# Nystromformer attention and multiplicative FFN: padded q tiles for the rest of A's scores, one load for the first w3 block, constants made at once, a q/k ring of four, and new due times

## The chip, the cores and the metric

The kernel runs on one core of a Trainium2 chip. A time is the device time of one execution, in microseconds; the time of a kernel is the median of its runs. The core has five engines with an instruction stream each: TensorE (PE in the profile; PEld is its weight load), VectorE (DVE), ScalarE (ACT), GpSimd (POOL) and SyncE (SP), which here only issues DMAs. GpSimd and, for the last stores, ScalarE issue DMAs too. Each stream is executed in its own order, and semaphores tie the streams together.

## The reference

Batch 8, 8 heads, sequence 576, head size 64, 32 landmarks. The result of the attention, 4608 tokens by 512, goes through a feed-forward block without a nonlinearity but with an elementwise product.

```python
q_lm = q.reshape(B, H, 32, 18, D).mean(axis=3)       # landmarks: means over 18 rows
k_lm = k.reshape(B, H, 32, 18, D).mean(axis=3)
A  = softmax(q @ k_lm.T / 8)                         # 576 x 32
Bm = softmax(q_lm @ k_lm.T / 8)                      # 32 x 32
C  = softmax(q_lm @ k.T / 8)                         # 32 x 576
Z  = Bm.T / (norm_1(Bm) * norm_inf(Bm) + 1e-6)
for _ in range(6):
    Z = 2 * Z - Z @ Bm @ Z
x  = (A @ Z @ C @ v)                                 # heads side by side: 4608 x 512
out = ((x @ w1) * (x @ w2)) @ w3 @ w_out             # 512 -> 1024 -> 1024 -> 512
```

## The kernel before, in words

**Work.** The kernel never forms x. It multiplies w3 by w_out once ("w34", 1024 x 512) and, for each batch, folds w1 and w2 into the small matrix Z C v ("U"), so that the dense part needs two products only: A times U (d1_mm, 768 products of 192 columns) and the elementwise product of its two halves times w34 (d2_mm, mostly of 512 columns).

**A quad** n (16 of them) is four heads of a batch: n = 2b + qd. For each quad, GpSimd issues two DMAs that load q and k and cast them to 16 bits into a tile "nat" (load_qk, L415); VectorE transposes both halves in blocks of 32 into Tq and Tk (trans, L444); the landmark means are made on TensorE for the first two quads (mean_mm) and on GpSimd for the others (mean_a, mean_b, mean_c, L452 to L467), turned into lmT (L490). Then come C's scores (s_mm) with Bm's scores beside them, A's scores (a_mm), softmaxes and A's transposition (a_trans, a_copy). The 576 rows of a head are 32 landmarks times 18 rows r; a_mm takes r = 0 to 15 in four groups of four rows, so 128 columns of Tq each. Two rows are left over, r = 16 and 17. For the two quads of a batch a_rest does them together (L239 with tile wide<-lmT,Tq, shape 128*64): four products, each on half of the array's columns, quad 0 into the lower and quad 1 into the upper half of the output's partitions, two accumulation steps each.

**A lane** g (pair_tasks) takes two batches: softmax of Bm, its norms, five iterations (it_mm, it_sq, it_out), Z, and the small product W. u_tasks makes U from W and the weights w1 and w2, which GpSimd loads (load_w12, L436).

**w34.** w3 comes in eight blocks of 512 KB (load_w3, L315), w_out in eight chunks of 256 KB (load_wout, L310), all issued by SyncE. A block is transposed on TensorE (w3_tr, L333), split into a high and a low 16-bit part by ScalarE (L340) and VectorE (L347); a chunk is split likewise (L320, L325); then 24 products of 512 columns per block follow, in groups of three for each chunk c (w34_mm, tiles bank<-wo,u). The first block is loaded and transposed in pieces of 1, 3 and 4 column groups, the others in halves of 4.

**Constants.** const_a (VectorE, zeros) and const_b (GpSimd, cb: the 128 x 128 identity) come first. const_c (VectorE, masks and ones, L273 to L284) must not start before 6.0 in the planner's time; const_d (ScalarE, L287 to L291) follows it. const_e are GpSimd's zero fills of v tiles (L296).

**Order.** A list scheduler (class Plan) writes all streams' order when the kernel is built. Each task has an engine, an estimated duration, dependencies, ring slots that it takes and frees, a due time ("prio") and sometimes an earliest time ("after"). On each engine the task that could start first is taken; among tasks that could start together, that with the lowest due time. On TensorE, a task in the array shape that is in use gets a bonus (MP for the full array, MT for the tiled shapes "64x32", "128x32", "32x32", "128x64"), because a change of shape costs INTO and OUT. The due times come from T0 + PER * b for the dense work of batch b, from att(n) for quads, lane(g) for lanes, cvt(b) for C times v, UO for U, p0 for a w3 block. Rings: six PSUM banks, six nat tiles, four Tq tiles and others.

Of the kernel before, what the change touches and what calls it, by code (L numbers as in the profile page):

```python
# [25 lines left out]
MT = 12.0  # L26
# [15 lines left out]
class Plan:  # L42
# [48 lines left out]
    def run(self):  # L91
# [15 lines left out]
        while len(order) < n:  # L107
            best = None
            for e, cand in avail.items():
# [7 lines left out]
                if not opts:  # L117
# [4 lines left out]
                    o[1].prio - ((MP if mode == "full" else MT) if e == "PE" and o[1].mode == mode else 0.0)))  # L122
# [43 lines left out]
def kernel(  # L166
# [13 lines left out]

    fixed = ctx.enter_context(tc.tile_pool(name="fixed", bufs=1))
# [14 lines left out]
    nats = slots(fixed, 6, [128, 2, GRP, D], FP16, "nat")  # L196
    Tqs = slots(fixed, 4, [128, GRP, M, 2], FP16, "Tq")
# [15 lines left out]
    bscs = slots(fixed, 2, [128, 4, 32], FP32, "bsc")  # L213
    wTs = slots(fixed, 2, [128, 2, 256], FP16, "wT")
    cvs = slots(fixed, 4, [128, 2, D], FP32, "cv")
    bms = slots(fixed, 2, [128, 4, 32], FP32, "bm")
    xzs = slots(fixed, 3, [128, 4, 2, 32], FP32, "xz")
    zbs = slots(fixed, 1, [128, 4, 4, 32], FP32, "zb")
# [22 lines left out]


    T0 = 66.0
# [5 lines left out]
    def att(n):  # L249
        first = dense(2 * (n // 4)) - 53.0 + 7.5 * (n % 4)  # L250
        return max(3.0 + 6.0 * n, first)

    def lane(g):
        return dense(2 * g) - 26.0

    def cvt(b):
        return lane(b // 2) - 0.0 + 3.0 * (b % 2)
# [3 lines left out]
    UO = 2.0  # L261
# [105 lines left out]

    def w34_tasks():
        for j in range(8):
            p0 = 4.0 + 8.6 * j  # L370
            cuts = [(0, 1), (1, 4), (4, 8)] if j == 0 else [(0, 4), (4, 8)]
            acq = [("w3n", f"w3n{j}", 1, len(cuts))]
            if j == 0:
                for h, (c0, c1) in enumerate(cuts):
                    add(f"wm{h}" if h else "w3n0", "SP", 0.43, load_w3(0, 128 * c0, 128 * c1),
                        acq=[] if h else acq, prio=(-0.01, 0.105, 0.115)[h], move=0.183 * (c1 - c0), lat=2.0)
            else:
                add(f"w3n{j}", "SP", 0.43, load_w3(j), acq=acq, prio=0.125 if j == 1 else p0 - 8.0,
                    after=0.0 if j == 1 else max(0.0, p0 - 12.0), move=1.46, lat=2.0)
# [8 lines left out]
            for h, (c0, c1) in enumerate(cuts):  # L388
                acq = [("P", f"ptr{j}{h}", 1, 2)]
                if h == 0:  # L390
# [3 lines left out]
                    deps=["cb", f"wm{h}" if h and j == 0 else f"w3n{j}"] + ([f"tr{j}{h - 1}"] if h else []), acq=acq,  # L394
# [46 lines left out]
    def trans(n, t):  # L441
        def fn():
            T = Tks[at(f"Tk{n}")] if t else Tqs[at(f"Tq{n}")]
            nc.vector.transpose(  # L444
                out=T.rearrange("p r l e -> p (r l e)").bitcast(FP32),
                in_=nats[at(f"nat{n}")][:, t].rearrange("p r d -> p (r d)").bitcast(FP32))
# [76 lines left out]
    def b_out(n):  # L523
        def fn():
            b, qd = divmod(n, 2)
            r, o = slice(64 * qd, 64 * qd + 64), 2 * (b % 2)
            nc.vector.tensor_copy(out=bscs[at(f"bsc{b // 2}")][r, o:o + 2, :],
# [45 lines left out]
    def a_mm(n):  # L573
        def fn():
            T, lm, ps = Tqs[at(f"Tq{n}")], lmTs[at(f"lmT{n}")], a_bank(n)
            for i in range(4):
                for e in range(2):
                    mm(ps[:, 128 * i:128 * i + 128], T[:, 4 * i:4 * i + 4, :, e], lm[:, 4:8, :, e],
# [73 lines left out]
    def quad_tasks(n):  # L652
# [9 lines left out]
        add(f"tq{n}", "DVE", 0.7, trans(n, 0), deps=loads, acq=[("Tq", f"Tq{n}", 1, 2)],  # L662
# [21 lines left out]
        if qd:  # L684
            add(f"R{b}", "PE", 0.14, a_rest(b), deps=[f"A{n}", f"tq{n - 1}", f"lt{n - 1}"],
# [442 lines left out]
```

## Time and profile before

| | us |
|---|---|
| median of 3 runs | 281.22 (280.86 to 283.8) |
| profiled execution | 281.59 |
| its span, first to last instruction | 279.8 |
| TensorE busy | 264.4 |
| VectorE busy | 195.0 |
| ScalarE busy | 167.2 |
| GpSimd busy | 141.9 |
| share of 16 DMA engines, SyncE's queue / GpSimd's queue | 29.3% / 23.7% |

The span is the time from the first to the last instruction; the rest of the execution lies around it. In the rows of slices each digit is a fortieth of the span (7 us), in tenths. In rows of groups a tile name out<-in stands for what an instruction writes and reads, with the shape, the number of instructions, their busy time and the mean in ns; busy times of products overlap, because products are pipelined, so the time that one takes from the next is read from the starts. A row of the timeline or of the chain gives the start in us, the duration in us and the engine.

### The profile page before, as it was taken

How to read it: one execution, taken by the hardware profiler on the slowest of the kernel's cores; microseconds unless marked ns; L12 is line 12 of the kernel's file. 1: busy time of each engine (PE TensorE's matmuls, PEld its weight loads, DVE VectorE, ACT ScalarE, POOL GpSimd, SP SyncE). 2: the span in 40 equal slices, each digit the busy share in tenths (PEclk: the TensorE clock that was granted, in tenths of full speed). 3: DMA queues.
4: the chain of work that ended last, by engine and by line, in shares of the span. 5: the costliest groups of instructions: out<-in, count | busy, mean ns of one | idle time of the engine just before them, and what ended most of it. 6: DMA issues, size and time to landing. Idle time of an engine off the chain costs nothing.

```text
span 279.8 us, 9998 instructions
## 1 busy us (share of the span) xinstructions
PE 264.4 (94%) x4116; PEld 177.3 (63%) x4116; DVE 195.0 (70%) x514; ACT 167.2 (60%) x457; POOL 141.9 (51%) x183
## 2 busy tenths in 40 slices
PE   3799999988999999999999899999999999999993
PEld 1456566744647767776676666756776665775762
DVE  2669995978858999779979757777883462442540
ACT  4643453424467776567986177599746667768551
POOL 8902999987998979989898920121010000000000
PEclk9999999999999999999999999999999999999998
DMA  6999995999935564789832751211211112121223
GB/s 176 316 316 270 256 286 116 232 219 215 187 66 87 86 124 127 171 234 184 178 98 89 180 156 40 76 39 41 77 41 42 40 45 71 63 89 40 77 76 112
DMA packets 19181, 37.34 MB, mean 133 GB/s; under 512 B 2880, under 2 KB 3392, under 8 KB 19136
## 3 DMA queue, kind: packets, MB, share of 16 engines
q1 hardware_dynamic: 13136, 24.91, 29.3%
q0 software_dynamic: 5760, 11.54, 23.7%
q8 instruction: 32, 0.52, 0.8%
q10 hardware_dynamic: 240, 0.26, 0.3%
q14 instruction: 13, 0.11, 0.1%
HBM read 38.80 MB, written 9.44 MB: 172 GB/s over the span
## 4 chain that ended last, share of the span: by engine, by line
PE 80%; DVE 12%; DMA 2%; issue 2%; ACT 1%; SPq 1%; DVEq 0%
PE bank L239 73%; PE wide L239 4%; DVE ab L965 3%; DMA osb<-in_moe_w_dram 2%; PE bank L333 2%; DVE bank L747 1%; PE bank L635 1%; DVE tiny L598 1%; DVE ea L604 1%; DVE ecT L563 1%; DVE tiny L520 1%; DVE tiny L619 1%; DVE Tq L444 1%; DVE Tk L444 0%; SPq L310 0%
## 5 line engine op out<-in xcount | busy, mean ns | idle before, releaser
L239 PEld LDWEIGHTS <-u 128*128 128x128 f16 x960 | 81.3, 99 | 32.2 <-issue 8.1
L965 DVE TENSOR_TENSOR ab<-asb,bank 128x192 f16<-128x192 f16 x192 | 60.2, 347 | 38.4 <-ACT asb L959 37.9
L239 PE MATMUL bank<-aT,u 128*128 128x192 f16 x768 | 78.2, 247 | 0.3 <-DVE ab L965 0.3
L239 PE MATMUL bank<-w,ab 128*128 128x512 f16 (+1 forms) x296 | 73.4, 374 | 0.8 <-issue 0.8
L959 ACT CAST asb<-bank 128x192 f16<-128x192 f32 x192 | 57.5, 329 | 22.9 <-PE bank L239 19.4
L239 PE MATMUL bank<-wo,u 128*128 128x512 f16 x192 | 50.5, 395 | 0.0
L459 POOL TENSOR_TENSOR ls<-ls 128x128 f32<-128x128 f32 (+2 forms) x56 | 40.8, 728 | 3.6
L239 PEld LDWEIGHTS <-ab 128*128 128x128 f16 x296 | 26.9, 98 | 22.0 <-issue 3.8
L452 POOL TENSOR_TENSOR ls<-nat 128x1152 f32<-128x1152 f16 x14 | 33.3, 2382 | 12.5 <-DVE Tk L444 12.1
L881 ACT CAST u<-bank 128x512 f16<-128x512 f32 x64 | 35.2, 599 | 6.4 <-PE bank L239 6.2
L626 POOL TENSOR_TENSOR ah<-ea,tiny 128x512 f16<-128x512 f32 (+1 forms) x16 | 18.5, 1159 | 37.9 <-ACT u L881 16.5
L991 ACT ACTIVATE osb<-bank 128x512 f32<-128x512 f32 x35 | 21.2, 605 | 12.7 <-PE bank L239 12.5
L547 ACT ACTIVATE ec<-wide,tiny 128x288 f32<-128x288 f32 x32 | 15.8, 501 | 9.1 <-DVE tiny L540 9.0
L239 PE MATMUL bank<-w,wT 64*32 64x512 f16 x512 | 18.9, 380 | 0.0
L239 PE MATMUL bank<-vb,ecT 128*32 128x128 f32 x576 | 17.9, 273 | 0.0
L340 ACT ACTIVATE u<-bank 128x512 f16<-128x512 f32 (+2 forms) x17 | 9.7, 569 | 12.2 <-PE bank L333 8.5
L467 POOL TENSOR_TENSOR lm<-ls,meanS 128x256 f16<-128x256 f32 x28 | 16.6, 617 | 0.4
L239 PE MATMUL bank<-xz 32*32 32x64 f32 (+1 forms) x768 | 15.1, 213 | 1.6 <-DVE cv L737 1.4
L239 PEld LDWEIGHTS bank<-xz 32*32 32x32 f32 x768 | 11.2, 105 | 7.5 <-issue 2.4
L815 ACT COPY xz<-bank 128x128 f32<-128x128 f32 x16 | 4.3, 269 | 19.3 <-PE bank L239 19.1
L239 PEld LDWEIGHTS bank<-vb,ecT 128*32 128x32 f32 x576 | 15.7, 110 | 0.3 <-issue 0.2
L563 DVE STREAM_TRANSPOSE ecT<-ec 128x576 f32<-128x576 f32 x16 | 12.1, 756 | 3.6 <-ACT ec L547 3.6
(93 smaller groups left out, 325.2 us busy)
## 6 DMA issues: line engine op xcount, KB each, us to landing
vb<-in_v_dram SPq DMA_DIRECT2D x64, 144.0 KB, 5.0
out_dram<-osb SPq DMA_DIRECT2D x37, 128.0 KB, 2.3
nat<-in_k_dram POOLq DMA_DIRECT2D x16, 288.0 KB, 5.1
nat<-in_q_dram POOLq DMA_DIRECT2D x16, 288.0 KB, 7.0
out_dram<-osb SPq DMA_DIRECT2D x16, 256.0 KB, 3.0
w3n<-in_moe_w_dram SPq DMA_DIRECT2D x4, 512.0 KB, 10.9
w<-in_moe_w_dram POOLq DMA_DIRECT2D x8, 256.0 KB, 6.4
osb<-in_moe_w_dram SPq DMA_DIRECT2D x3, 512.0 KB, 6.9
```

Of the source, the lines that this page charges most:

```text
L239: nc.tensor.matmul(out_, lhsT, rhs, start=start, stop=stop, **({} if pos is None else {"tile_position": pos}))
L340: nc.scalar.activation(out=w3t[at(f"w3t{j}")][:, 0, 128 * c0:128 * c1], in_=bank(at(f"ptr{j}{h}"))[:, 0:128 * (c1 - c0)], func=AXF.Copy, s ...
L452: nc.gpsimd.tensor_tensor(out=l, in0=nat[:, :, 0:9, :], in1=nat[:, :, 9:18, :], op=ALU.add)
L459: nc.gpsimd.tensor_tensor(out=l[:, :, x:x + m, :], in0=l[:, :, x:x + m, :], in1=l[:, :, y:y + m, :], op=ALU.add)
L467: nc.gpsimd.tensor_tensor(out=lm[:, 4 * t:4 * t + 4, :], in0=l[:, t, 0, :].unsqueeze(1).to_broadcast([128, 4, D]), in1=meanS.unsqueeze(2). ...
L547: nc.scalar.activation(out=ecs[at(f"ec{n}")][:, hp, :, :].rearrange("p c x -> p (c x)"), in_=psS[:, hp, 0:HALF], func=AXF.Exp, scale=SCALE ...
L563: nc.vector.transpose(out=ecTs[at(f"ecT{n}")].rearrange("p a c x -> p (a c x)"), in_=ecs[at(f"ec{n}")].rearrange("p a c x -> p (a c x)"))
L626: nc.gpsimd.tensor_tensor(out=ahs[at(f"ah{n}")][:, 0:g, :], in0=eas[at(f"ea{n}")][:, 0:g, :], in1=tinies[at(f"ta{n}")][:, 0:g].unsqueeze(2 ...
L881: nc.scalar.copy(out=uu[at(f"u{b}{qd}")][:, wi, 512 * half:512 * half + 512], in_=bank(at(f"pU{b}{wi}{half}{qd}")))
L959: nc.scalar.copy(out=asb[at(f"as{b}{j}{th}")], in_=bank(at(f"pD{b}{j}{th}"))[:, 0:THIRD])
L965: nc.vector.tensor_mul(ab[:, j, c0:c0 + THIRD], asb[at(f"as{b}{j}{th}")], bank(at(f"pD{b}{j}{th}"))[:, THIRD:2 * THIRD])
L991: nc.scalar.activation(out=osb[at(f"os{t}")], in_=bank(at(f"pE{t}")), func=AXF.Copy, scale=2.0 ** -12)
```

## The change

- **Rest of A's scores.** The Tq tiles get two zero rows r ahead and two behind (18 + 4 rows in all). Quad 0's rows stand at 2 to 19, so that its window 18 to 21 holds rows 16 and 17 and then zeros. Quad 1's rows 0 to 15 stand at 4 to 19 and its rows 16 and 17 at 2 and 3, so that window 0 to 3 holds zeros and then these rows; its transposition becomes two instructions. a_rest then does four products on the full array into the same 128 x 128 output, all in one accumulation; zeros keep the two quads apart. Its mode is "full" in the planner, its estimate 0.22 instead of 0.14. The zero rows are written once by GpSimd, in eight memsets (task "tp"), which wait for nothing; the first a_rest waits for them.
- **First w3 block.** One load of 512 KB in place of three; its transposes are still three tasks.
- **Constants.** const_c has no earliest time any more, and const_c and const_d have due times -5 and -4 in place of 5 and 6.
- **Ring.** Four nat tiles in place of six.
- **Order.** T0 is 68 for 66, MT 11 for 12, the step of p0 8.3 for 8.6; lane(g) and U keep their due times, since their offsets grow by the 2 that T0 grows; attention quads and dense work are due 2 later, the w1/w2 loads 1 earlier. A second bonus MY, for going from one tiled shape to another, is added with the value 0.
- **Groups.** pair_tasks becomes group_tasks, which can take groups of more than two batches. GR is 2, so the groups are the pairs of before, tiles keep their sizes, and the instructions are the same; a few estimates move by 0.02 to 0.1.

The core of the diff (the group functions, which do the same work at GR = 2, are left out):

```diff
-MT = 12.0
+MT = 11.0
+MY = 0.0
+GR = int(2.0)
...
-                    o[1].prio - ((MP if mode == "full" else MT) if e == "PE" and o[1].mode == mode else 0.0)))
+                    o[1].prio - (0.0 if e != "PE" else (MP if mode == "full" else MT) if o[1].mode == mode
+                                 else MY if "full" not in (mode, o[1].mode) else 0.0)))
...
-    nats = slots(fixed, 6, [128, 2, GRP, D], FP16, "nat")
-    Tqs = slots(fixed, 4, [128, GRP, M, 2], FP16, "Tq")
+    nats = slots(fixed, 4, [128, 2, GRP, D], FP16, "nat")
+    Tqs = slots(fixed, 4, [128, GRP + 4, M, 2], FP16, "Tq")
...
-    T0 = 66.0
+    T0 = 68.0
...
     def att(n):
-        first = dense(2 * (n // 4)) - 53.0 + 7.5 * (n % 4)
-        return max(3.0 + 6.0 * n, first)
+        bs = GROUPS[GOF[n // 2][0]]
+        k = n - 2 * bs[0] - 2 * len(bs) + 4
+        first = dense(bs[0]) - 53.0 + 7.5 * k
+        return max(12.0 + 6.0 * n, first)
 
     def lane(g):
-        return dense(2 * g) - 26.0
+        return dense(GROUPS[g][0]) - 28.0
...
-    UO = 2.0
+    UO = 4.0
...
+    def pads():
+        for T in Tqs:
+            nc.gpsimd.memset(T[:, 0:2], 0.0)
+            nc.gpsimd.memset(T[:, GRP + 2:GRP + 4], 0.0)
+
+    add("tp", "POOL", 1.0, pads, prio=1.0)
...
-    add("cc", "DVE", 1.7, const_c, deps=["cb"], prio=5.0, after=6.0)
-    add("cd", "ACT", 1.0, const_d, deps=["cc"], prio=6.0)
+    add("cc", "DVE", 1.7, const_c, deps=["cb"], prio=-5.0)
+    add("cd", "ACT", 1.0, const_d, deps=["cc"], prio=-4.0)
...
+    W1 = 3.0
+    FIRST = [(0, 1), (1, 4), (4, 8)]
+    PIECES = [(0, 8)]
...
-            p0 = 4.0 + 8.6 * j
+            p0 = 4.0 + 8.3 * j
...
-                for h, (c0, c1) in enumerate(cuts):
+                for h, (c0, c1) in enumerate(PIECES):
                     add(f"wm{h}" if h else "w3n0", "SP", 0.43, load_w3(0, 128 * c0, 128 * c1),
-                        acq=[] if h else acq, prio=(-0.01, 0.105, 0.115)[h], move=0.183 * (c1 - c0), lat=2.0)
+                        acq=[] if h else acq, prio=-0.01 + h * 0.11, move=0.183 * (c1 - c0), lat=2.0)
...
     def trans(n, t):
         def fn():
             T = Tks[at(f"Tk{n}")] if t else Tqs[at(f"Tq{n}")]
-            nc.vector.transpose(
-                out=T.rearrange("p r l e -> p (r l e)").bitcast(FP32),
-                in_=nats[at(f"nat{n}")][:, t].rearrange("p r d -> p (r d)").bitcast(FP32))
+            parts = [(0, 0, GRP)] if t else [(4, 0, 16), (2, 16, 18)] if n % 2 else [(2, 0, GRP)]
+            for to, r0, r1 in parts:
+                nc.vector.transpose(
+                    out=T[:, to:to + r1 - r0].rearrange("p r l e -> p (r l e)").bitcast(FP32),
+                    in_=nats[at(f"nat{n}")][:, t, r0:r1].rearrange("p r d -> p (r d)").bitcast(FP32))
...
     def a_rest(b):
         def fn():
-            for e in range(2):
-                for qd in range(2):
-                    n = 2 * b + qd
-                    mm(psS[64 * qd:64 * qd + 64, 1, 0:128], Tqs[at(f"Tq{n}")][:, 16:18, :, e],
-                       lmTs[at(f"lmT{n}")][:, 4:8, :, e], start=(e == 0), stop=(e == 1),
-                       pos=(0, 64 * qd))
+            for qd in range(2):
+                T, lm = Tqs[at(f"Tq{2 * b + qd}")], lmTs[at(f"lmT{2 * b + qd}")]
+                cut = slice(0, 4) if qd else slice(GRP, GRP + 4)
+                for e in range(2):
+                    mm(psS[:, 1, 0:128], T[:, cut, :, e], lm[:, 4:8, :, e], start=(qd == 0 and e == 0),
+                       stop=(qd == 1 and e == 1))
...
-            add(f"R{b}", "PE", 0.14, a_rest(b), deps=[f"A{n}", f"tq{n - 1}", f"lt{n - 1}"],
-                rel=[f"Tq{n}", f"Tq{n - 1}", f"lmT{n}", f"lmT{n - 1}"], prio=p + 0.3, mode="128x64")
+            add(f"R{b}", "PE", 0.22, a_rest(b), deps=[f"A{n}", f"tq{n - 1}", f"lt{n - 1}", "tp"],
+                rel=[f"Tq{n}", f"Tq{n - 1}", f"lmT{n}", f"lmT{n - 1}"], prio=p + 0.3, mode="full")
...
-                add(f"lw{s}{qd}{wi}", "POOL", 0.62, load_w12(s, qd, wi), prio=T0 - 10.0 + qd, after=T0 - 10.0 - 4.0,
+                add(f"lw{s}{qd}{wi}", "POOL", 0.62, load_w12(s, qd, wi), prio=T0 - 13.0 + qd, after=T0 - 13.0 - 4.0,
```

More of the change, by code (lines that the diff above doesn't have):

```diff
@@ L753, in fn @@
         def fn():
-            ps = bank(at(f"pN{g}"))[:, 0:128]
-            nc.scalar.activation(out=ps, in_=ps, func=AXF.Exp, scale=SCALE)
+            nc.scalar.activation(out=quarter(g, 0), in_=quarter(g, 0), func=AXF.Exp, scale=SCALE)
         return fn
@@ L865, in fn @@
         def fn():
-            wT, f, o = wTs[at(f"wT{b // 2}")], slice(512 * half, 512 * half + 512), 128 * (b % 2)
+            g0, i0 = GOF[b]
+            wT, f, o = wTs[at(f"wT{g0}")], slice(512 * half, 512 * half + 512), 128 * i0
             ps = [bank(at(f"pU{b}{wi}{half}{qd}")) for qd in range(2)]
@@ L925, in pair_tasks @@
-        add(f"wq{g}", "DVE", 0.8, w_out(g), deps=[f"W{g}"], acq=[("wT", f"wT{g}", 1, 8)],
-            rel=[f"pY{g}"], prio=p + 12.3)
+        q += step * 5
+        add(f"Z{g}", "PE", 0.02 + 0.26 * k, z_mm(g), deps=last, acq=[("P", f"pZ{g}", 1, 1)], rel=[f"xz{g}_5"],
+            prio=q, mode="32x32")
+        add(f"zo{g}", "DVE", 0.06 + 0.54 * k, z_out(g), deps=[f"Z{g}"], acq=[("zb", f"zb{g}", 1, 1)],
+            rel=[f"pZ{g}"], prio=q + 0.3)
+        add(f"W{g}", "PE", 0.03 + 0.44 * k, w_mm(g), deps=[f"zo{g}"] + [f"co{b}" for b in bs],
+            acq=[("P", f"pY{g}", 1, 1)], rel=[f"zb{g}"] + [f"cv{b}" for b in bs], prio=q + 1.0, mode="128x64")
@@ L928, in u_tasks @@
+        add(f"wq{g}", "DVE", 0.15 + 0.65 * k, w_out(g), deps=[f"W{g}"], acq=[("wT", f"wT{g}", 1, 4 * len(bs))],
+            rel=[f"pY{g}"], prio=q + 1.3)
     def u_tasks(b):
@@ L1075 @@
         cv_tasks(b)
-    for g in range(B // 2):
-        pair_tasks(g)
+    for g in range(len(GROUPS)):
+        group_tasks(g)
     for b in range(B):
```

190 lines of the change are left out of this document (99 added, 91 removed).

## The prediction

> **What bounds the kernel now.** I read the page's busy table and slices first, then the chain in order of time, then single engines' timelines.
>
> ```profile
> PE 264.4 (94%) x4116; PEld 177.3 (63%) x4116; DVE 195.0 (70%) x514; ACT 167.2 (60%) x457; POOL 141.9 (51%) x183
> ...
> PE   3799999988999999999999899999999999999993
> ...
> POOL 8902999987998979989898920121010000000000
> PEclk9999999999999999999999999999999999999998
> DMA  6999995999935564789832751211211112121223
> ```
>
> TensorE (PE) is short of work in the first slice only (a slice is 7 us) and a little around 50 to 70 us; from 212 us it alone is the chain. So a microsecond counts if it takes work or a hole from TensorE. GpSimd (POOL) is nearly full from 26 to 100 us, and the 16 DMA engines from 7 to 40.
>
> The chain in order of time shows the two kinds of hole:
>
> ```profile
> 3.57 6.24 DMA osb<-in_moe_w_dram
> 9.85 1.11 PE bank L333 x4
> ...
> 65.19 0.25 PE wide L239 x7
> 65.45 1.15 issue
> 66.60 0.32 PE wide L239 x7
> ```
>
> Up to 9.85 us it is the second w3 block's landing. Later, "issue" holes: at 65.15, 57.92, 100.76, 159.11 and 163.85 TensorE stops for 1.45, 1.55, 0.46, 1.00 and 0.47 us beyond its step (4.9 in all). Each follows a packet of the instruction queue (q8); four times TensorE goes on 1.41 to 1.44 us after that packet's end, the fifth time 1.64. I read them as late instruction blocks. Only three holes of 0.26, 0.32 and 0.94 us are waits for VectorE (DVE) in the softmax of Bm.
>
> Third, TensorE's timeline: the same form, three products of 512 columns, early and later.
>
> ```profile
> 10.76 1.49 PE L239 MATMUL bank<-wo,u 128*128 128x512 f16 x3
> ...
> 21.28 0.81 PE L239 MATMUL bank<-wo,u 128*128 128x512 f16 x3
> ```
>
> From start to start one takes 427 ns until 15.03 us and 216 ns after, though the PEclk row reads 9 throughout. TensorE is unbroken from 9.85 us, so it took 5.2 us of unbroken work to reach full pace. By 15.03 it had done 16 transposes and 11 products, worth 16 x 0.107 + 11 x 0.213 = 4.06 us at full pace.
>
> **The change part by part. Start.** Today the first piece of w3 (64 KB) lands at 2.73 us, but its use ends in holes: product group c=1 stands behind the second block's transposes, which wait until 9.85, though its operands were ready at 8.85. After the change all 512 KB come first, w_out's chunks behind. By the packets of before, 0.52 MB have started by 4.07 and 0.79 MB by 5.06 us, and landings came 0.4 to 1.5 us behind; so the block lands near 4.5 (3.6 to 4.7) and chunk 0 near 5.7 (4.7 to 6.6). Eight transposes run from 4.5 to 6.2. Chunk 0 needs ScalarE (0.63, L320) and VectorE (0.69, L325): the first product starts near 7.1. Chunks 1 and 2 land near 6.8 and 7.7, the second block near 9.5; each group of three takes 1.28 us at the slow pace, so TensorE is unbroken from 7.1. If full pace again needs 5.2 us, it comes at 12.3, and by 15.03 the work done is 0.86 + 5.2/2 + 2.73 = 6.2 us against 4.06: a lead of 2.1; I take -2.0. Bounds: full pace still at 15.03 gives 0.86 + 7.9/2 = 4.8, a lead of 0.8; at 10.3 it is 7.2, a lead of 3.1. Enough work is there: blocks 0 and 1 hold 16 groups, of which 9 are done by 18.3 today. The page "TensorE: Matmul & The Clock Gate" of the Trainium skill (Part 1) says the clock doubles after one busy window of about 3.4 us that runs freely; 5.2 us lies between one and two windows, so the trace agrees. By that rule an estimate for the doubling is 10.5 to 13.9 us, and the sum would be 0.9 us lower to 0.8 higher.
>
> **Zero pads, in front on GpSimd.** The eight memsets wait for nothing, so the planner puts them first, ahead of the identity (cb) and everything GpSimd does after it.
>
> ```profile
> 1.32 4.32 POOL L296 MEMSET vb<- 64x1152 f32 x4
> 5.59 0.72 POOL L415 DMA_DIRECT2D nat<-in_k_dram  x1
> ...
> 26.46 2.37 POOL L452 TENSOR_TENSOR ls<-nat 128x1152 f32<-128x1152 f16 x1 [12.12 <-DVE Tk L444]
> ```
>
> L296 takes 1052 ns for 1152 elements, so 128 elements cost 0.11 to 0.2 us, the eight 0.9 to 1.6; I take 1.2. The identity moves from 1.38 to about 2.6, hidden, as w3 lands at 4.5. The constants on VectorE (1.54 us) and ScalarE (1.37) then end near 5.5, just ahead of chunk 0; without that cover the first product slips 0.5. Before, the VectorE part ran at 6.72, where chunk 1 waited 0.9 us for it. The q/k loads are issued 1.2 later. In the last row GpSimd had idled 12 us; the real releaser is quad 2's q, landed at 26.29. Its queue is served in order and had a gap of 1 us only, so I expect 27.4. GpSimd's row of work then starts 1.1 late; A's first normalization (an0, ends 29.98) feeds transposes at 30.56, so 0.6 is covered: +0.5 on TensorE (0 to 1.2). Later rows: the load of quad 4, issued 2 us later by its due time, landed at 42.52 for use at 45.82: covered. The w1/w2 loads, due 1 us earlier, may put four issues (4 x 0.62) ahead of quad 5's mean (mc5); it ends at 64.5 for products at 75.54: covered.
>
> **Rest of A's scores.** Twice from the table of groups by form and once from the timeline:
>
> ```profile
> L239 PE MATMUL wide<-lmT,Tq 128*128 128x128 f16 x64 | 5.0, 219 | 0.0
> L239 PE MATMUL wide<-lmT,Tq 128*64 128x128 f16 x32 | 2.4, 231 | 0.0
> ...
> 144.01 0.31 PE L239 MATMUL wide<-lmT,Tq 128*64 128x128 f16 x4
> ```
>
> The durations agree; the starts matter. Four half-array products hold TensorE 0.24 us (the next starts at 144.25), and the last full-array step ahead is 92 ns longer than its like. Full-array products follow each other at 57 ns: 4 x 0.057 = 0.23. So -0.10 for the six between full-array work; the two between other tile shapes lose 0.08 to 0.10, as the switch stays. If all eight get full neighbours it is -0.8, as now placed -0.4; I take -0.6. The Trainium skill speaks against this edit: "TensorEngine Tiling (Array Packing)", Performance Considerations, has column tiling for outputs of 64 columns, up to 2x faster. The trace disagrees, since the 0.24 is mostly the 0.15 us end of the last product.
>
> **Odd q transposes in two.** Tq takes 751 ns for 576 elements, lmT 431 for 256: 1.0 ns each plus 0.175. Less 0.07 of overlap, a second piece adds 0.1, eight times. VectorE is the chain from 90 to 103 us and hidden elsewhere by TensorE: +0.2 (0 to 0.8).
>
> **Ring of four.** Every q/k load of before was issued after the last reader of the load four earlier; closest is load 15 (135.9 against 133.15). Zero, and load 15 landed 14 us ahead of its first use.
>
> **New order.** Dense and attention are due 2 us later, w3 blocks up to 2.1 earlier, lanes and U as before; the group functions do the same work at groups of two. No TensorE work goes; what can change is holes and tile switches. Of 4.9 + 1.5 us of holes I take none away and none more: 0, with -2.9 (two long holes gone) and +5.8 (four more) as ends.
>
> **Sum**: -2.0 + 0.5 - 0.6 + 0.2 = -1.9 against the profiled execution's 281.59 (span 279.8 and 1.8 around it): 279.7. The median of the runs shown is 0.4 lower, so 279.3 beside 281.22.
>
> **Rivals.** *The order closes holes*: of the five instruction holes two long ones go (2.9): 276.4. For it: they hang on where short products crowd. Against: all that crowds stays. *The lead is lost*: loads land at their late ends, or GpSimd's lateness stops TensorE at A's transposes, +1.2 and a lead of 0.8: -0.8 + 1.2 - 0.6 + 0.2 = 0, 281.2. For it: only 0.6 us of cover. *The start isn't changed*: full pace at 15.03 again, so 0.8 instead of 2.0: 280.5. *Slower: late instruction blocks.* Each costs up to 1.45 us; two more than now cancel the gain, four more give 279.3 + 5.8 = 285.1. For it: 32 blocks are fetched over DMA engines that are full to 75 us, and new order puts U, x and score products, 32 to 64 instructions in under half a microsecond, elsewhere. Against: late in the kernel DMA is quiet. *Half-array pairs were a gain*: if full-array products cost double the old 0.24 us, +1.9 in place of -0.6: 281.8. The step of 57 ns speaks against it. It is the rule of the Trainium skill's "TensorEngine Tiling (Array Packing)".
>
> **How the numbers follow.** Forecast 0.40 (its own range 277.8 to 280.8); holes closed 0.22; lead lost 0.09; start unchanged 0.08; late blocks 0.18; pairs 0.03. About 1% (2.8 us) is what can be told from no change. Below 278.4 lie the closed holes and a quarter of the forecast: 0.32. Above 284.0 lies most of the late blocks: 0.16. Within: 0.52. The range 276.0 to 284.4 leaves out the farther half of each outer case.
>
> **What would show it.** Step 216 ns for 512 columns from about 12.3 us; TensorE unbroken from 7.1; quad 2's q landing near 27.4 and no hole over 1 us at A's first transposes; R as four products 57 ns apart; five "issue" holes. Wrong if the first product starts after 9 us, if the holes sum to over 8 us or under 3, or if GpSimd waits for a ring slot.

## The result and the profile after

The changed kernel takes 278.94 us (median of 20 runs) beside 281.73 for the kernel before (20 runs on the same chip): ratio 0.9886, 95% interval 0.986 to 0.9912, so 1.1% faster, where 0.7% was forecast. Ratios and intervals, here and below, are of the executions within 1.5% of the fastest of their kernel; medians are of all. The profiled execution took 278.2 us with a span of 276.3 (before: 281.59 and 279.8).

The busy table and three rows of slices, after:

```profile
PE 260.7 (94%) x4116; PEld 178.3 (65%) x4116; DVE 194.4 (70%) x522; ACT 165.0 (60%) x457; POOL 143.3 (52%) x191
...
PE   3989999998999997999999999999999999999993
...
POOL 9920999999789999967899950121100000000000
PEclk9999999999999999999999999999999999999999
DMA  6999993999955546399665751211210221221223
```

TensorE is still the bound. The second slice went from 7 to 9, which is the start; GpSimd's idle slices (2 and 0, 14 to 27.6 us) end with the landing of quad 2's q at 26.80, and the DMA engines are full from 7 to 41 us as before.

TensorE's timeline over the first 17 us, after (start, duration, engine, line, operation, tiles, shapes, count, idle time ahead):

```profile
4.70 1.94 PE L351 MATMUL bank<-ident,osb 128*128 128x128 f32 x8 [4.70 <-DMA osb<-in_moe_w_dram]
6.44 2.77 PE L243 MATMUL bank<-wo,u 128*128 128x512 f16 x6
...
9.69 0.81 PE L243 MATMUL bank<-wo,u 128*128 128x512 f16 x3
...
10.77 4.70 PE L243 MATMUL bank<-wo,u 128*128 128x512 f16 x21
16.46 1.18 PE L243 MATMUL bank<-nat,ident 128*128 128x128 f16 x18 [0.99 <-DMA nat<-in_q_dram]
```

One load brings all eight transposes at 4.70 and the first product at 6.44 us; the three products at 9.69 take what three took at 21.28 before, so full pace is there 5 us after the first transpose. But at 15.5 us TensorE runs out of w34 products and waits 1 us for q of quad 0, a wait that the kernel before did not have.

TensorE's waits, after (total us, number, longest):

```profile
PE bank L351 <- DMA osb<-in_moe_w_dram: 4.7, 1, 4.7
PE bank L243 <- DMA nat<-in_q_dram: 1.6, 2, 1.0
PE wide L243 <- issue: 1.5, 1, 1.5
PE bank L243 <- DVE xz L856: 1.5, 1, 1.5
PE bank L660 <- POOL ah L651: 0.9, 2, 0.5
PE bank L243 <- DVE bank L801: 0.5, 1, 0.5
...
```

Of the "issue" holes one long one is left, at 106.55 us; in the chain in order of time of the profile after it stands between two runs of products:

```profile
100.27 6.45 PE bank L243 x210
106.84 1.54 issue
108.71 9.03 PE bank L243 x219
```

To see where the time went I summed the steps of TensorE (start of one product to start of the next) of both profiles. A step is its form's usual step, plus a usual excess where the array's shape changes, plus the rest, called a hole where it is over 0.2 us.

| us | before | after |
|---|---|---|
| until the first product's step is normal: idle and half pace | 10.9 | 7.0 |
| usual steps | 205.7 | 207.4 |
| changes of array shape (141 / 125) | 20.6 | 17.9 |
| holes after the start | 7.6 | 8.8 |
| small excess and tail | 35.1 | 35.1 |
| span | 279.8 | 276.3 |

The start gave 3.9, twice the forecast. R gave four full-array steps for each pair, hence the 1.7 more of usual steps, and sixteen changes of shape fewer. The holes grew by 1.2: those that the prediction calls instruction blocks fell from 4.9 to 2.1, while waits for q, k and GpSimd that were not there before take 3.1 (1.16 at 15.1, 0.70 at 21.4, 0.61 at 29.9 and again at 38.8), and waits for lanes grew by about 1. This table alone would name the start as the cause. The experiments do not bear that out.

### The profile page after: what moved, and what is told of

Same layout as the page of the kernel before. It is cut to its first block, busy times and chain, and to the rows that moved or that the text cites. A ratio compares the mean times of both kernels' runs of the same rounds, so it can differ in the third digit from the quotient of the medians.

```text
span 276.3 us, 10013 instructions
## 1 busy us (share of the span) xinstructions
PE 260.7 (94%) x4116; PEld 178.3 (65%) x4116; DVE 194.4 (70%) x522; ACT 165.0 (60%) x457; POOL 143.3 (52%) x191
## 4 chain that ended last, share of the span: by engine, by line
PE 70%; DVE 10%; POOL 8%; DMA 7%; issue 2%; ACT 1%; POOLq 0%; DVEq 0%; ACTq 0%
PE bank L243 65%; DMA nat<-in_q_dram 7%; PE wide L243 3%; POOL vb L308 3%; DVE ab L1002 2%; POOL ah L651 1%; PE bank L660 1%; POOL nat L437 1%; POOL ls L483 1%; POOL ls L476 1%; DVE bank L786 1%; DVE tiny L623 1%; DVE ea L629 1%; DVE tiny L644 1%; DVE Tq L468 1%
## 5 line engine op out<-in xcount | busy, mean ns | idle before, releaser
L243 PE MATMUL bank<-wo,u 128*128 128x512 f16 x192 | 49.9, 388 | 0.0
L468 DVE STREAM_TRANSPOSE Tq<-nat 128x576 f32<-128x576 f32 (+2 forms) x24 | 12.6, 550 | 5.1 <-DMA nat<-in_q_dram 5.1
L243 PEld LDWEIGHTS bank<-vb,ecT 128*32 128x32 f32 x576 | 15.5, 110 | 0.1
L638 ACT ACTIVATE ea<-ea 128x512 f32<-128x512 f32 (+1 forms) x16 | 11.0, 688 | 7.1 <-DVE ea L629 7.1
```

Source lines behind the costliest of these rows:

```text
L243: nc.tensor.matmul(out_, lhsT, rhs, start=start, stop=stop, **({} if pos is None else {"tile_position": pos}))
L468: nc.vector.transpose(out=T[:, to:to + r1 - r0].rearrange("p r l e -> p (r l e)").bitcast(FP32), in_=nats[at(f"nat{n}")][:, t, r0:r1].rear ...
L638: nc.scalar.activation(out=ea, in_=ea, func=AXF.Exp, scale=SCALE)
```

## The experiments

In three_loads, consts_late, warm, loads_first, pads_late, half_rest and phase the order of the changed kernel is kept but for the edit; the other kernels are planned anew. Ratios are to the kernel before on the same chip.

### Is it the start?

**start_only**: the kernel before, planned anew with two edits.

```diff
-                for h, (c0, c1) in enumerate(cuts):
-                    add(f"wm{h}" if h else "w3n0", "SP", 0.43, load_w3(0, 128 * c0, 128 * c1), ...
+                add("w3n0", "SP", 0.43, load_w3(0), acq=acq, prio=-0.01, move=1.46, lat=2.0)
...
-    add("cc", "DVE", 1.7, const_c, deps=["cb"], prio=5.0, after=6.0)
+    add("cc", "DVE", 1.7, const_c, deps=["cb"], prio=-5.0)
-    add("cd", "ACT", 1.0, const_d, deps=["cc"], prio=6.0)
+    add("cd", "ACT", 1.0, const_d, deps=["cc"], prio=-4.0)
```

> The kernel before with two edits alone: the first w3 block in one load, and the constants due at once; order of the rest planned with the old due times, ring of six, half-array R, no pads. Theory 'the start is worth its 3.9 us less what q and k take back': w3 lands near 3.6, the first transpose is near 3.7, the first product near 5.5, the 427 ns step ends near 8.7, and the time is 279 to 280.5 against 281.9 of the kernel before (ratio .990 to .995). Rival 'all of it is in the start': 278 to 278.5 (ratio .986). Rival 'the start is absorbed by q and k': 281.5 to 282 (ratio 1.00).

Measured: 282.1 us beside 282.67, ratio 0.9984 (0.9956 to 1.0013). The third theory held for the ratio: nothing measurable. The start itself is there: first product at 6.38 us and full pace by 10.1. TensorE's waits and a piece of its timeline in this run show where it goes:

```profile
PE bank L333 <- DMA osb<-in_moe_w_dram: 4.6, 1, 4.6
PE bank L239 <- issue: 3.5, 2, 2.6
PE bank L633 <- POOL ah L624: 2.0, 1, 2.0
PE bank L239 <- DMA nat<-in_q_dram: 0.7, 1, 0.7
...
```

```profile
21.48 1.18 PE L239 MATMUL bank<-nat,ident 128*128 128x128 f16 x18 [0.72 <-DMA nat<-in_q_dram]
...
30.27 0.41 PE L633 MATMUL bank<-ident,ah 128*128 128x128 f16 x4 [2.02 <-POOL ah L624]
30.50 1.46 PE L239 MATMUL bank<-wo,u 128*128 128x512 f16 x3
31.75 1.06 PE L333 MATMUL bank<-ident,w3n 128*128 128x128 f32 x4
32.61 1.47 PE L239 MATMUL bank<-wo,u 128*128 128x512 f16 x3
```

TensorE is early at the second quad's means and at A's first transposes, and stands there for q and for GpSimd, whose adds wait for q of quad 2 (landed at 26.52 us; 26.29 before). After the halt of 2.2 us before 30.27 (from start to start) three products take 1.47 instead of 0.81, half pace again.

The granted clocks on record tell more of this. Profiles that hold a stretch of half clock (granted 0.50 for 3.4 us, last section) have a mean granted clock of 0.984 to 0.994, the others of 0.997 to 1.000. Ten of start_only's twelve executions are at 0.994 or less, but only two of 17 of the kernel before beside them. The other two of start_only took 280.3 and 280.4 us, 2.0 less than the median of the 15 others of the kernel before (282.4). Two executions are few; they suggest that the start is worth what was forecast while the clock stays full, and that half clock after the long halts takes most of it back.

**three_loads** and **consts_late** undo the two edits in the changed kernel, order kept.

```diff
+    P.by["w3n0"].fn = load_w3(0, 0, 128)      # then columns 128:512 behind wf0, 512:1024 behind wf1
...
+    move("cc", "wl01")      # consts_late: VectorE's constants behind its second w3 split,
+    move("cd", "wh02")      # ScalarE's behind its third
```

> The changed kernel with its order kept on all compute engines, only w3's first block comes in three loads again (64, 192 and 256 KB with w_out's first chunks between, as before). The third piece then lands near 7.6 us, and as all eight transposes stand ahead of the first product, that one starts near 8.5 instead of 6.4. Theory 'the lead counts in full': +2.0, 280.9. Rival 'most of the lead is given back in waits for q and k': TensorE waits 1.16 us at 15.1 and 0.7 at 21.4 us for q landings and 0.6 twice for GpSimd; being later by 2 us it finds these done, so +0.2 to +0.8, 279.1 to 279.7.

> The changed kernel with its order kept, only the constants of VectorE and ScalarE stand where they stood before the change (VectorE's behind the second split of w3's first block, ScalarE's behind the third). They delay w_out's chunk 1 by 1.5 us on VectorE and chunk 3 by 1.4 on ScalarE; the second product group starts near 9 instead of 7.7 us. Theory 'waits for q and k absorb it': 0 to +0.3, 278.9 to 279.2. Rival 'every part of the start counts': +1.0, 279.9.

Measured: 279.27 us, ratio 0.9922 (0.9887 to 0.9956), and 280.1 us, ratio 0.9909 (0.9867 to 0.9951), beside 0.9886 with both. With three loads the first product comes at 9.05 instead of 6.44 us, yet the last w34 product of block 7 starts at 85.69 instead of 84.99: of 2.6 us 0.7 is left by then. The holes at 15.1, 21.4 and 29.9 are gone, that at 38.8 stays. With late constants the first product is even earlier (6.17) and the first dense product comes at 87.67 (87.58 in the changed kernel). By the ratios the two edits are worth 0.4% and 0.2% here, and both intervals overlap that of the changed kernel. For three_loads that is the rival; the 0.2% of consts_late lies between its theory and its rival.

**warm** takes the start further the other way: nine products on zeros, which nobody reads, ahead of everything on TensorE.

```diff
+    nc.vector.memset(warm, 0.0)
+    for i in range(9):
+        mm(psS[:, i % 2, :], warm[:, 0:128], warm)
```

> The changed kernel with nine products of 512 columns on a tile of zeros, which nobody reads, on TensorE from about 0.8 us on, its order otherwise kept; const_a comes one DVE fill (about 0.2 us) later. Theory 'the start is given back at q and k': the 427 ns step ends near 5.5 instead of 9.7, some eleven products run 0.21 us faster, TensorE reaches the first score group 2.3 us earlier, and the waits for q of quads 0 and 1 (1.16 and 0.70 us after the change) grow to 3.5 and 0.7 us: the time is 278.4 to 279.2, no better than the changed kernel by more than 0.5. Rival 'each us at the start counts': 276.5 to 277 (ratio to the kernel before .980).

Measured: 278.88 us, ratio 0.989 (0.9848 to 0.9932), the time of the first theory, but not its way. Full pace comes by 6.4 us instead of 9.7, and TensorE then stands 1.4, 0.5 and 0.4 us between 6.6 and 9.8 for w_out's splits and the second w3 block, and 1.1 us at 21.4 for q. So most of this lead is lost before q matters.

**loads_first** asks whether q and k could come earlier.

```diff
+    move("tp", "lq3")       # pads, and the two late constants, behind the load of quad 3
+    move("ce3", "lq3")
+    move("ce2", "lq3")
```

> The changed kernel with its order kept but for three GpSimd steps (the fill of the pad of t, and the two late constants) moved behind the load of q and k of quad 3, so that quads 1 to 3 are issued up to 2 to 3 us earlier. Theory 'q and k are the path after the start': q of quads 1 and 2 lands 1 to 2 us earlier, the holes at 21.4, 29.9 and 38.8 (0.70, 0.61, 0.61 us after the change) go, that at 15.1 stays, and the time is 277 to 278.2 (ratio .982 to .986). Rival 'the transfers share the same DMA engines with the w3 blocks': q of quad 1 lands less than 0.5 us earlier, w3's last block later, and the time stays at 278.6 to 279.4.

Measured: 279.56 us, ratio 0.9871 (0.9839 to 0.9904): no gain that can be told. In its profile (281.39 us, the slowest of six executions) quads 1 to 3 are issued 5.2 us earlier, and their q lands at 21.03, 25.85 and 30.27 instead of 22.18, 26.80 and 31.78: 1.0 to 1.5 us for 5.2. In the thirteen other profiles, with first products between 5.4 and 9.1 us, q of quad 3 lands between 30.8 and 32.3. So the landings follow neither the issue nor TensorE's start, and the profile shows the DMA engines full until 41 us. That these landings pace TensorE's first 40 us is argued from this and from the waits above; no run moved them further.

### Is it the pads ahead of q and k?

**pads_late** moves only the fill of the pads behind quad 3's load, order kept; **old_pads_late** does so with every old due time.

```diff
+    move("tp", "lq3")
```

> The changed kernel with its order kept, only the eight zero fills of the q tiles are moved on GpSimd behind the load of quad 3's q and k, where GpSimd idles until 27 us anyway. The identity and the q/k loads come 1.2 us earlier. Theory 'issue time sets the landing': q of quads 0, 1 and 2 lands 1.0 to 1.2 us earlier, TensorE's waits at 15.1, 21.4, 29.9 and 38.8 us shrink from 3.1 to about 1.5 in sum: -1.0, 277.9. Rival 'full DMA engines set it': landings within 0.4 us of now, 278.9.

> The changed kernel with every old due time of the planner, and the GpSimd fill of the pads moved behind the loads of q and k of quads 0 to 3 (order of the rest kept). Theory 'the pads ahead cost the first q and k about a microsecond': as in the run of the pads moved alone (278.34, ratio .986, beside .9886), q of quads 0 and 1 lands 1 us earlier (15.1 and 21.2 instead of 16.4 and 22.2), the hole near 15 goes, and the time is 277 to 277.7 (ratio .980 to .983). Rival 'given back later': as the old due times alone, 278.1 to 278.8 (ratio .984 to .987).

Measured: 278.34 us, ratio 0.986 (0.9819 to 0.99), and 277.83 us, ratio 0.9851 (0.9798 to 0.9903; old due times alone: 0.9848). q of quads 0 to 2 lands 1.3, 1.0 and 0.5 us earlier, the hole at 15.1 goes and that at 29.9 grows from 0.61 to 1.10. The landings are those of the first theory, but the four waits shrink by 0.6 us only, not by half. The first dense product comes 0.5 us earlier, as the +0.5 of the forecast has it; in the whole time it cannot be told from nothing. "Given back later" is nearer in the second run.

### Is it the rest of A's scores?

**half_rest** puts the half-array products back, reading the padded tiles, order kept.

```diff
-                cut = slice(0, 4) if qd else slice(GRP, GRP + 4)
+                r0 = 2 if qd else GRP
                 for e in range(2):
-                    mm(psS[:, 1, 0:128], T[:, cut, :, e], lm[:, 4:8, :, e], ...
+                    mm(psS[64 * qd:64 * qd + 64, 1, 0:128], T[:, r0:r0 + 2, :, e], lm[:, 4:8, :, e], ..., pos=(0, 64 * qd))
```

> The changed kernel with its order of all instructions kept, only the rest of A's scores is again four products on half of the array's columns (same padded q tiles). If the change of array shape is what it costs (0.24 us held by the four, plus 0.092 on the full-array step ahead, against 4 x 0.057), each of the eight takes 0.10 us more: +0.8, 279.7 against the changed kernel's 278.9, with eight more changes of shape in the trace. If the halves side by side were a gain of up to two, it is faster than the changed kernel, 277.5 to 278.5. If the time is absorbed by later waits: 278.9.

Measured: 279.89 us, ratio 0.9916 (0.9884 to 0.9947) beside 0.9886, so +0.9 us by the medians of the two, at the edge of what can be told. The steps of the two profiles give the form itself little: shape changes +1.8 us (140 for 125), usual steps -1.7, so +0.1. Of the 1.8 us between the two profiles 1.5 stand in 3.4 us of half clock from 69.8 us, which the changed kernel's has not. So the +0.8 that was expected of the change of shape is not shown, though the time fits it. The Trainium skill's "TensorEngine Tiling (Array Packing)", Performance Considerations, names 2x column tiling for a left side of 64 columns; here going back to it gained nothing, and the trace decides.

**rest_only** is the complement of start_only: pads, full-array R and the ring of four, planned anew, but three loads, late constants and every old due time. The estimates of the changed kernel stay.

```diff
-    PIECES = [(0, 8)]
+    PIECES = FIRST
...
-    add("cc", "DVE", 1.7, const_c, deps=["cb"], prio=-5.0)
+    add("cc", "DVE", 1.7, const_c, deps=["cb"], prio=5.0, after=6.0)
...
-    T0 = 68.0
+    T0 = 66.0
```

> The complement of the run with the start alone: zero-padded q tiles with the rest of A's scores as full-array products, ring of four, and the planner as changed, but the first w3 block in three loads, the constants due where they were before (5 and 6 us), and every old due time. It holds the padding and R without the start and without the new order. Theory 'the gain lies in R and in where the instruction blocks fall': the start alone gave 282.1 beside 282.67, so this gives 279 to 280 (ratio to the kernel before .985 to .990), nearly the whole gain. Rival 'start and R are worth something only together, as q and k arrive': 281 to 282.5 (ratio .995 to 1.00).

Measured: 277.59 us beside 282.26, ratio 0.9847 (0.9798 to 0.9896). The whole gain is there without the start and without the new due times, against the second theory. All of TensorE's waits that the view lists:

```profile
PE bank L351 <- DMA osb<-in_moe_w_dram: 5.7, 4, 2.9
PE bank L351 <- ACT xz L846: 0.9, 1, 0.9
PE bank L660 <- POOL ah L651: 0.6, 1, 0.6
PE bank L243 <- DVE bank L801: 0.4, 1, 0.4
PE bank L243 <- DVE ab L1002: 0.3, 1, 0.3
```

The slow start of the kernel before is unchanged (5.7 us in four waits, first product at 5.47, half pace until 14.9), but no "issue" wait is left in the list (the wait put to ScalarE's xz stands at a block's edge, below), and the holes after the start sum to 3.6 us (7.6 before). Split at the first dense product, the spans of the profiles are:

| us | start to first dense product | from there to the end | shape changes, usual steps and holes of that second part |
|---|---|---|---|
| before | 89.2 | 190.6 | 15.2, 144.3, 4.5 |
| start_only | 92.0 | 189.9 | 15.4, 144.3, 2.9 |
| ring4_only | 90.5 | 190.8 | 15.2, 144.3, 3.7 |
| rest_only | 88.0 | 187.5 | 13.7, 145.4, 1.8 |
| old_due | 89.5 | 187.6 | 14.1, 145.4, 2.0 |
| old_pads_late | 88.1 | 187.7 | 14.1, 145.4, 2.2 |
| changed kernel | 87.6 | 188.7 | 13.3, 145.4, 3.7 |

The first parts of start_only and ring4_only hold two stretches and one stretch of half clock, 3.4 us each; no second part in the table holds one ahead of its last few us. Under the old due times all three kernels with padded R need 187.5 to 187.7 us for the second part, and all three with half-array R 189.9 to 190.8. Against the kernel before, R's steps with their shape changes are 0 to 0.4 us of these 3, and holes 2.3 to 2.7.

The holes differ because TensorE's order differs, and that order hangs on three entries of the planner: R's shape and estimate, the odd q transposes' estimate (0.77 for 0.7) and that of a lane's first step (`ba`, 0.6 for 0.5). With these put back, rest_only's list of TensorE's 491 tasks is the list of the kernel before; R's shape, R's estimate or either of the other two alone already changes it. No run tells them apart, so that R in full shape brings the better order is not shown.

### Is it the order, and what are the "issue" holes?

**old_due** puts all old due times into the changed kernel; **ring4_only** changes one number in the kernel before. Both are planned anew.

```diff
-    T0 = 68.0
+    T0 = 66.0
-        return max(12.0 + 6.0 * n, first)
+        return max(3.0 + 6.0 * n, first)
...
-    nats = slots(fixed, 6, [128, 2, GRP, D], FP16, "nat")      # ring4_only, in the kernel before
+    nats = slots(fixed, 4, [128, 2, GRP, D], FP16, "nat")
```

> The changed kernel with every due time of the kernel before put back into its planner (T0 66, MT 12, 8.6 a group of heads, lane -26, UO 2, A's groups from 3 + 6n, the late weights at T0 - 10), so that zero pads, first block in one load, early constants, ring of four and full-array R stay and only the order is another. Theory 'order counts': the profiles gave TensorE 141 changes of array shape before and 125 after, 20.6 us beside 17.9; with the old due times some 140 changes and the long holes for instruction blocks (4.9 us before, 2.1 after) come back, and the time is 281 to 283. Rival 'start only': the time is that of the changed kernel within 1 us, 278.5 to 279.9.

> The kernel before with one size changed: four q/k tiles instead of six, the order planned anew with that. Theory 'the ring costs nothing' (the step of the prediction put it at 0): 282 to 283 (ratio .997 to 1.003). Rival 'the ring of four makes loads late': the load of quad 4 waits for the adds of quad 0, q and k of later quads land after they are wanted, and the time is 283.5 to 285 (ratio 1.004 to 1.01).

Measured: old_due 278.14 us, ratio 0.9848 (0.9814 to 0.9883), the rival: the due times bring none of the gain. Its 127 changes of shape against 125 show that the fewer changes do not come from them either. rest_only (0.9847) differs from it in the start alone, so in that order too no worth of the start can be told; the intervals allow some 1.4 us either way. ring4_only 281.92 us, ratio 0.9996 (0.9968 to 1.0024): the ring costs nothing, and TensorE's list of tasks is that of the kernel before.

**phase** has 48 products of one column, which nobody reads, ahead of the changed kernel's, order kept.

```diff
+    for i in range(48):
+        mm(psS[:, 0, 0:1], warm[:, 0:128], warm[:, 0:1])
```

> The changed kernel with 48 products of one column on a tile of zeros, which nobody reads, ahead of everything on TensorE; order otherwise kept. Theory 'holes at instruction blocks': in all runs of this order TensorE halts before its 1494th product (106.55 us, 1.83 us, after an instruction packet at 106.13); the block's edge stays at that number, so the halt comes 48 products earlier in the work, inside the small lane products near 105.4 (in the run with nine products ahead it came at number 1494 too), or shrinks under 1 us as another stretch of work precedes it; and the hole before product 799 (67.56, 1.5 to 1.9 us), which the waits put to VectorE, is not found before product 847. Rival 'the holes are waits for data': they stay before the same work, numbers 847 and 1542. Time: 277 to 281, either sign.

Measured: 279.59 us, ratio 0.9919 (0.9891 to 0.9947). The run was made for the place of the holes, not for the time. Its profile has a halt of 3.4 us at 14.6 us, before product 94, which is an edge too; q of quad 0 landed 0.05 us before its end (17.93), so which of the two it was cannot be told. TensorE's timeline of this run around the hole, and then that of the changed kernel:

```profile
105.60 0.53 PE L243 MATMUL bank<-xz 32*32 32x64 f32 x22
108.08 0.41 PE L243 MATMUL bank<-xz 32*32 32x64 f32 x10 [1.95 <-issue]
```

```profile
105.08 0.65 PE L243 MATMUL bank<-xz 32*32 32x64 f32 x32
105.66 1.06 PE L243 MATMUL bank<-w,wT 64*32 64x512 f16 x32
106.54 0.30 PE L243 MATMUL wide<-Tk,lmT 64*32 64x288 f16 x6
108.38 0.43 PE L243 MATMUL wide<-Tk,lmT 64*32 64x288 f16 x10 [1.54 <-issue]
```

The halt moved from the middle of a run of score products into the middle of a run of lane products, 48 products earlier in the work: in both it is after the 1494th product that TensorE has started, as in the six other runs of this order, warm with its nine extra products too. In the orders planned with the old due times the halts that follow a packet lie after numbers 602 or 603, 731, 2384 and 2513; there the waits name another engine at times, as in rest_only after number 602. The 32 packets of the instruction queue hold 16 KB each for 4116 products, so about 128 products a packet, and these numbers, 1494 among them, lie whole multiples of 127.3 apart, within two. So these holes are block edges. Two others are not. The hole at 67.56 went from number 799 to 847, with its work, against the expectation, so it is the wait for VectorE that the view names. And the smallest of the prediction's five, 0.46 us at 100.76, lies after number 1267, some 27 products past an edge; there TensorE's timeline names VectorE:

```profile
101.44 0.49 PE L239 MATMUL bank<-aT,u 128*128 128x192 f16 x4 [0.30 <-DVE ab L965]
```

Whether an edge halts TensorE depends on when its packet comes. After the edge before, at 103.35 us, the packet of the changed kernel began only at 106.13, with q and k of quad 11 under way (landed 103.89 and 105.92); TensorE did its 127 products in 3.2 us and stood until 108.38. In rest_only the packet began 0.4 us after that edge, and there was no halt. In the kernel before, the packet of the halt at 65.15 began 6.0 us after the edge before it. At edges of the changed kernel with no transfer under way, it was 0.56 (96.46) and 0.11 us (200.90). What holds a packet back is not shown: at rest_only's edge four loads of v were under way too.

Half clock bears on the order as well. Of the changed kernel's 20 executions nine have a mean granted clock of 0.994 or less, of the 18 of old_due, rest_only and old_pads_late two. The medians of the others are 278.1 us against 277.9, 277.6 and 277.6, so a good part of what the new due times seem to cost goes with half clock; the kernels ran on different chips, so its size is not settled.

## Why the prediction was right in the number and wrong in the cause

**Forecast 279.3, measured 278.94**, inside the forecast's own range. Its sum was -2.0 for the start, +0.5 pads, -0.6 R, +0.2 transposes, 0 order. By the same steps:

- **Start, -2.0: the step that failed.** Its timing was cautious: block landed at 4.57 (4.5 forecast), first product at 6.44 (7.1), full pace at 9.69 (12.3), 3.9 us in the profile. But its worth at the end is 0.5 us in one order (start_only's ratio; interval -0.4 to +1.2), none in another (old_due beside rest_only), some 0.4% for the load in the third. Only two of start_only's executions, those without half clock, show the full 2.0. The forecast assumed that a lead on TensorE lasts as long as w34 products are there to do. The cover was counted in products, not against the landing of q, though the page's DMA row stood at 9 from 7 to 40 us. The mechanism of the rival "the lead is lost", TensorE stopped at A's transposes, is what happened in start_only, and half clock after such a halt, which no rival has, added to it.
- **Pads, +0.5**: the direct effect is right (first dense product 0.5 us earlier without them). The eight fills took 1.2 us as forecast; q of quad 2 landed at 26.80 (27.4). What was not forecast is the wait for q of quads 0 and 1 (1.16 and 0.70); pads_late takes the first away, three_loads both, so it needs the earlier start and the later loads together.
- **R, -0.6**: products follow each other at 57 to 59 ns as forecast; undoing the form costs 0.1 by its steps and 0.9 by the medians. The sign held; the size lies between and is not settled.
- **Transposes, +0.2**: 693 and 200 ns for 756, in rows that overlap. Right in size; no run measured it alone.
- **Ring, 0**: right (ratio 0.9996).
- **Order, 0: failed too.** Its own sign of failure came true, however it is read: "issue" holes of 2.1 us, under 3, and 8.8 us of holes in all, over 8. Of the 4.9 us of instruction holes that it started from, 0.46 was a wait for VectorE. The rival "the order closes holes" has its mechanism shown in part: the halts at edges 603, 731, 2384 and 2513 of the kernel before are not in the changed kernel's profile. They are not fixed, though: with the same list for TensorE, ring4_only has none at 731, and five of the seven other runs of the changed order have one of 0.3 to 1.1 us at 603, 2384 or 2512. Halts at edges sum to 4.4, 3.6 and 3.9 us in the three profiles with half-array R and old due times, and to 1.0, 2.1 and 2.2 in the three with padded R. But the prediction looked for this in the due times. It comes with the order that padded R and the new estimates give: rest_only has it, old_due has it, start_only and ring4_only have not. The new due times then bring a halt at 1494, which the old ones have not, and half clock after it in some executions; 0.4% by the ratios of old_due and the changed kernel, within the intervals.

So two errors met. Everything but the start and the due times was put at +0.1 and gave -4.3 us (rest_only's ratio; interval -2.9 to -5.7); start and new due times together were put at -2.0 and, by the two ratios, took back 1.1 of that, which is within the intervals. The net was right by that chance. The table of steps above would not have shown it: it credits the start with 3.9 us and hides that halts which replaced it come with the early start: three of the four new ones are gone in three_loads.

**Open**: which placements in rest_only let each packet come in time, since no run moved only R in the list of the kernel before, or only the two estimates of VectorE; and whether R's form or the order carries the 3 us of the second part. half_rest speaks for the order: half-array products in the changed kernel's order need the same 188.7 us there, though with 1.1 us less of holes and 0.9 more of small excess. rest_only (0.9847) is the fastest median of all; that it beats the changed kernel (0.9886) is within the intervals. How much half clock takes from each start is open too, since the clock of most kernels is on record for few executions.

## What to carry to other kernels

A lead at the start is worth what the next scarce resource lets through: before crediting it, follow it to the first landing that the bound engine will need, here q of quads 0 to 3 over full DMA engines. Look at the granted clock of every execution, too: a gain can be lost to half clock that one profile does not show. Try each part of a change alone and left out, since a sum of profile differences cannot tell a wait that was caused from one that was merely moved. Where short products crowd on TensorE, count products to the next edge of an instruction block, and ask which transfers are under way there.

## What was not expected of the hardware

**A halt of 2 us can cost half pace afterwards.** Of the 24 halts of 1.0 to 1.85 us (from start to start) after 16 us in the fourteen profiles none was followed within 8 us by 512-column products at 427 ns; of the 15 halts from 2.0 to 2.8 us nine were. Stretches of pads_late after its halt of 2.12 us at 106.02 (columns: stretch, length, busy time and number of TensorE, of its weight loads, of VectorE, ScalarE and GpSimd, granted clock, share of the DMA engines, GB/s):

```profile
106.00:108.20 2.20, 0.37 (x22) 0.07 (x12) 0.01 (x1) 1.39 (x3) 2.04 (x4) 1.00 0.54 135
108.20:110.00 1.80, 1.80 (x54) 1.52 (x55) 0.91 (x2) 0.45 (x2) 1.76 (x1) 0.62 0.06 17
110.00:112.00 2.00, 2.00 (x10) 1.06 (x8) 1.90 (x6) 0.92 (x3) 1.89 (x2) 0.50 0.02 4
112.00:130.00 18.00, 18.00 (x305) 12.74 (x304) 14.10 (x37) 10.57 (x31) 13.36 (x19) 1.00 0.90 196
```

The granted clock falls to 0.50 after the halt is over, and comes back by 112 us. In the changed kernel's profile, with 1.83 us at the same place, it does not fall. Three runs of products behind the halt (32 of xz, eight of 192 columns, four of 512) take 1.00, 1.46 and 1.70 us here and 0.65, 0.83 and 1.03 there, 1.65 us more in all. The Trainium skill's "TensorE: Matmul & The Clock Gate", Part 1, gives an idle window of some 3.4 us as what brings the half clock; here a little over 2 us sufficed in nine of fifteen cases.

**The traces tell which cases.** In each trace all changes of the granted clock lie on one grid of 3.413 us, which starts elsewhere in each execution, and each of the ten stretches at 0.50 ahead of the last few us is one step of that grid. From the first change on, the fourteen traces hold 1068 such steps. TensorE is busy, by the profile's modelled ends, for less than half of the step (1.71 us) in 13 of them. Ten of these are followed by a step at 0.50; three (1.52, 1.68 and 1.69 us) are not, and none of the other 1055 is. So in these traces it is not the halt alone that counts but how its idle time falls on the grid. pads_late's step around the halt and the one behind it, and then the changed kernel's:

```profile
105.21:108.62 3.41, 1.58 (x64) 0.81 (x68) 0.78 (x5) 1.83 (x4) 3.13 (x5) 1.00 0.61 164
108.62:112.03 3.41, 3.41 (x44) 2.24 (x40) 2.80 (x7) 1.37 (x4) 3.25 (x3) 0.50 0.03 9
```

```profile
105.08:108.49 3.41, 1.87 (x82) 1.07 (x82) 1.43 (x5) 1.83 (x4) 3.10 (x6) 1.00 0.81 227
108.49:111.90 3.41, 3.41 (x99) 2.50 (x94) 2.81 (x7) 1.43 (x5) 3.26 (x2) 1.00 0.04 12
```
